# Head B's key blocks paired like head A's, and one block-diagonal product for both last blocks of a row tile

## The chip, the core and the metric

The kernel runs on one core of a Trainium2 chip. A core has a matrix engine (TensorE, PE in the profile; PEld is its loading of weights), a vector engine (VectorE, DVE), a scalar engine (ScalarE, ACT), a general engine (GpSimd, POOL) and a queue engine that only issues DMAs here (SyncE, SP). Each runs its own list of instructions in order, and they wait for each other through semaphores. On-chip memory is SBUF (128 partitions) and PSUM, into which PE writes. The metric is the time of one execution on the device, in microseconds.

## What is computed

Block-causal attention over 8 batches, 8 heads, 576 tokens and 64 channels, then a top-1 mixture of 8 experts. Cut to what matters:

```python
scores = q @ k.T / sqrt(64)                  # per batch and head, 576 x 576
mask   = block_i >= block_j                  # blocks of 64 tokens
attn   = softmax(where(mask, scores, -1e9))
x      = (attn @ v), heads side by side      # 4608 x 512
e      = argmax(x @ w_gate)                  # one expert a token
out    = gate * sigmoid(x @ w_output_gate)[e] * (relu(x @ w1[e]) @ w2[e])
```

The change lies in `attn @ v`. With blocks of 64 tokens, a query block i attends to key blocks 0 to i.

## The kernel before

**Pairs and weaves.** Two heads, A and B, of one batch make a pair; there are 32. The loop at L936 runs one `advance` a pair: it weaves the generators `softmax` of pair p, `flip` of pair p-1 and `values` of pair p-2, one round after another (a `yield` ends a round), and with them what stands in `later`: the loading of q and k for coming units of two pairs (`load_heads`), and a batch's `finish_batch`. This text calls one such pass weave p. PE's order is exactly that of the code. The other engines' lists come from a scheduler that weighs priorities, so an edit in one place can move their rows elsewhere.

**Row tiles.** Queries go in five row tiles: tile 0 holds block 0 (64 rows), tile t holds blocks 2t-1 and 2t (128 rows). `softmax` computes the scores of each tile against its 2t+1 key blocks, takes maxima on DVE (L351, L372, L383), scales them to biases (L327, L385) and writes the exponentials by ACT (L334) into `pt`: 64(2t+1) columns of A, then as many of B. PSUM for scores (`ps_s`) has two buffers.

**Transposes.** `flip` transposes `pt` in squares of 128 columns on PE (L402) and copies them into `pT` by ACT and DVE (L410). The columns fall into pairs of blocks: A's (0,1), (2,3), ..., then one mixed square, A's last block 2t beside B's block 0, then B's pairs (1,2), (3,4), .... So A has a block left at the end, B one at the start.

**Products with v.** `values` has the mixed squares first. v of the two heads comes for them in tiles padded with zeros: `vma` (rows 0 to 63 hold A's blocks 0, 2, 4, 6, 8, the others are zero) and `vmb` (rows 64 to 127 hold B's block 0). L417 and L418 are tile 0's, L421 is one product of 512 columns for B, L423 four of 128 for A. Then the pairs: `va` and `vb`, four products each, over 512, 384, 256 and 128 columns (L430, L434). A's results go to partitions 0 to 63, B's to 64 to 127; each product uses half of the array's columns, and an A and a B product run side by side. All sums gather in `ps_a`, which has one buffer; L441 copies it out, L419 the first tile's.

**Loads.** `load_v` issues four DMAs a pair on SP's queue, in runs of 256 bytes: va and vb (128 KB each), vma (80 KB), vmb (16 KB). The same queue carries q and k (`nat`, L91), their transposes by DMA (L102), the swapped copy of the keys (`sw`, L107 and L108), which the scores need, and the stores of x (L463). Between load and transpose, q and k are split into two f16 halves by DVE (L96) and POOL (L97).

**The batch's end.** `finish_batch` scales rows, routes tokens and ends in five indirect DMAs issued by POOL (L561, the scatters), ahead of the next splits in POOL's list.

Of the kernel before, what the change touches and what calls it, by code (L numbers as in the profile page):

```python
# [10 lines left out]
F32 = mybir.dt.float32  # L11
I32 = mybir.dt.int32
U32 = mybir.dt.uint32
AF = mybir.ActivationFunctionType
# [6 lines left out]
P = 128  # L21
# [5 lines left out]
def block_attention_top1_moe(  # L27
# [11 lines left out]
    nc = tc.nc  # L39
# [3 lines left out]
    NP = H // 2  # L43
# [155 lines left out]
    with tc.high_priority(offset=3000):  # L199
# [11 lines left out]
        vmb = [const.tile([P, D], F32, name=f"vmb{i}") for i in range(3)]  # L211
        vma = [const.tile([P, NT, D], F32, name=f"vma{i}") for i in range(3)]
        for i in range(3):
            nc.gpsimd.memset(vmb[i][0:64], 0.0)
            nc.gpsimd.memset(vma[i][64:128], 0.0)
# [82 lines left out]
    def load_v(b, hp):  # L298
        hA = 2 * hp
        par = (b * NP + hp) % 3  # L300
        va = sb.tile([P, 4, D], F32, name="va", bufs=3)
        vb = sb.tile([P, 4, D], F32, name="vb", bufs=3)
        nc.sync.dma_start(va, v[b, hA, 0:512].rearrange("(j p) d -> p j d", p=P))
        nc.sync.dma_start(vb, v[b, hA + 1, 64:576].rearrange("(j p) d -> p j d", p=P))
        nc.sync.dma_start(vma[par][0:64], v[b, hA].rearrange("(n p) d -> p n d", p=64)[:, 0:9:2, :])
        nc.sync.dma_start(vmb[par][64:128], v[b, hA + 1, 0:64])
        return va, vb, vma[par], vmb[par]

    def softmax(b, hp, stacks, h0, sums, probs):
# [19 lines left out]
        def exps(t, pieces):  # L329
            r, n = ROWS[t], NK[t]  # L330
            if t not in probs:
                probs[t] = sb.tile([P, 2 * n], F32, name=f"pt{t}")
            for ab, ap in pieces:
                last_exp[0] = nc.scalar.activation(  # L334
                    probs[t][0:r, ab * n:(ab + 1) * n], ap, AF.Exp,
                    bias=nbs[0:r, t, ab:ab + 1], scale=SCALE,
                    accum_out=sums[0:r, t, hA + ab:hA + ab + 1],
                )
# [52 lines left out]
    def flip(probs, pT):  # L391
# [4 lines left out]
        for g0 in range(0, len(slots), 4):  # L396
            grp = slots[g0:g0 + 4]
            ps = ps_t.tile([P, 512], F32, name="ps_t").rearrange("p (a n) -> p a n", n=P)
            for i, (t, r) in enumerate(grp):
                rows = ROWS[t]  # L400
                col = t if r == 0 else ((r - 1) // 2 if r % 2 else t + r // 2)
                nc.tensor.transpose(  # L402
                    ps[:, i, 0:rows], probs[t][0:rows, P * col:P * col + P], ident[0:rows, 0:rows]
                )
# [9 lines left out]
    def values(hp, pT, va, vb, vma, vmb, xT):  # L414

        pm = ps_t.tile([P, 512], F32, name="ps_t")
        nc.tensor.matmul(pm[0:64, 0:64], vma[:, 0, :], pT[:, 0, 0:64], start=True, stop=True)  # L417
        nc.tensor.matmul(pm[64:128, 0:64], vmb, pT[:, 0, 0:64], start=True, stop=True)  # L418
        nc.any.tensor_copy(xT[:, hp, 0:64], pm[:, 0:64])  # L419
        pa = ps_a.tile([P, 512], F32, name="ps_a")  # L420
        nc.tensor.matmul(pa[64:128, :], vmb, pT[:, 0, 64:576], start=True, stop=False)  # L421
        for t in range(1, NT):
            nc.tensor.matmul(  # L423
                pa[0:64, P * (t - 1):P * t], vma[:, t, :], pT[:, 0, Q0[t]:Q0[t] + P],
                start=(t == 1), stop=False,
            )
        yield
        yield
        for j in range(4):
            nc.tensor.matmul(  # L430
                pa[0:64, P * j:512], va[:, j, :], pT[:, 1 + 2 * j, 64 + P * j:576],
                start=False, stop=(j == 3),
            )
            nc.tensor.matmul(  # L434
                pa[64:128, P * j:512], vb[:, j, :], pT[:, 2 + 2 * j, 64 + P * j:576],
                start=False, stop=(j == 3),
            )
            if j % 2:
                yield
                yield  # L440
# [657 lines left out]
```

## Time and profile before

| | us |
|---|---|
| median of 3 runs (835.05 to 836.78) | 835.87 |
| the profiled execution | 833.94 |
| its span, first to last instruction | 831.9 |
| PE busy | 777.9 |
| VectorE busy | 547.4 |
| ScalarE busy | 517.4 |
| GpSimd busy | 261.1 |

```profile
## 2 busy tenths in 40 slices
PE   5599999999999999889996999999999999999995
...
DMA  8999889799999899983158499685789968822611
```

The slices are 20.8 us each: the first twenty are attention, the rest the experts. Each digit is the busy share in tenths. Rows of a time line give the start from the beginning of the span, the duration, engine, line, operation, output<-inputs, and in brackets how long the engine had been idle before and what ended that. Group rows give a count, the sum and the mean in ns. A window row gives its bounds, its length, the busy time and instructions of PE, PEld, DVE, ACT and POOL, PE's granted clock, the DMA share and GB/s.

### The profile page before, as it was taken

What the parts mean: (1) busy time and instruction counts of PE and PEld (TensorE: products, weight loads), DVE (VectorE), ACT (ScalarE), POOL (GpSimd) and SP (SyncE); (2) the same over time, 40 slices, a digit from 0 to 9 for tenths busy, and PEclk for the clock granted to TensorE, in tenths of its full rate; (3) what the DMA queues carried; (4) which work ended last, traced back from release to release, by engine and by line L of the source; (5) the groups of instructions that cost most, each with busy time, mean ns of one, the idle gap of its engine ahead of it and who ended that gap; (6) DMA issues with size and microseconds to landing.
All of it is one profiled execution on the core that took longest, in us unless ns stands there. A gap on an engine that the chain in (4) does not pass through costs nothing. (4 is left out here: it accounts for less than half of the span.)

```text
span 831.9 us, 17237 instructions
## 1 busy us (share of the span) xinstructions
PE 777.9 (94%) x6214; PEld 523.5 (63%) x6238; DVE 547.4 (66%) x1188; ACT 517.4 (62%) x1210; POOL 261.1 (31%) x233
## 2 busy tenths in 40 slices
PE   5599999999999999889996999999999999999995
PEld 3366666666676666555673766676656666776652
DVE  6467777878687777758561766786567656786540
ACT  4478786877778777666312855775555555775530
POOL 4322142424232243473236462223123222300001
PEclk9699999999999999999999999999999999999998
DMA  8999889799999899983158499685789968822611
GB/s 156 199 179 171 185 153 194 153 188 191 183 201 175 181 184 200 183 268 107 33 165 208 119 316 303 209 236 114 235 268 290 292 182 210 234 48 57 220 40 41
DMA packets 267053, 151.21 MB, mean 182 GB/s; under 512 B 235600, under 2 KB 235664, under 8 KB 266960
## 3 DMA queue, kind: packets, MB, share of 16 engines
q1 hardware_dynamic: 258688, 130.74, 68.6%
q0 software_dynamic: 8272, 19.29, 7.8%
q8 instruction: 51, 0.84, 0.4%
q14 instruction: 42, 0.34, 0.2%
HBM read 124.33 MB, written 19.73 MB: 173 GB/s over the span
## 5 line engine op out<-in xcount | busy, mean ns | idle before, releaser
L873 PEld LDWEIGHTS <-w1b 128*128 128x128 f16 (+1 forms) x2112 | 184.0, 98 | 26.5 <-issue 3.2
L873 PE MATMUL ps_s<-xt,w1b 128*128 128x256 f16 (+3 forms) x1824 | 182.1, 261 | 0.5 <-DVE w1b L763 0.4
L334 ACT ACTIVATE pt<-ps_s,nbs 128x448 f32<-128x448 f32 (+1 forms) x314 | 163.8, 531 | 23.9 <-DVE nbs L327 10.0
L900 PE MATMUL ps_t<-w2b,hh 128*128 128x512 f16 (+1 forms) x584 | 175.8, 379 | 2.3 <-ACT hh L881 2.3
L763 DVE TENSOR_TENSOR w2b<-w2f,w2b 128x1024 bf16<-128x1024 f32 x76 | 88.0, 1221 | 114.2 <-ACT w2b L762 114.2
L410 ACT COPY pT<-ps_t 128x512 f32<-128x512 f32 (+3 forms) x221 | 97.8, 463 | 74.1 <-PE ps_t L402 73.1
L402 PE MATMUL ps_t<-ident,pt 128*128 128x128 f32 (+1 forms) x800 | 133.0, 287 | 2.5 <-DVE xn L459 2.4
L900 PE MATMUL ps_t<-w2b,hl 128*128 128x512 f16 x304 | 115.2, 379 | 1.7 <-DVE hl L882 0.6
L97 POOL TENSOR_TENSOR sp<-nat,sp 128x1152 f16<-128x1152 f32 x30 | 71.2, 2375 | 145.1 <-DVE sp L96 111.2
L903 ACT ACTIVATE ys<-ps_t,ids 128x512 f32<-128x512 f32 x38 | 26.0, 688 | 137.7 <-PE ps_t L900 91.5
L319 PE MATMUL ps_s<-tr,tr 128*128 128x448 f16 (+1 forms) x378 | 99.6, 286 | 6.4 <-ACT pt L334 6.0
L900 PEld LDWEIGHTS <-hh 128*128 128x128 f16 x608 | 59.2, 98 | 69.2 <-ACT hh L881 2.8
L904 POOL DMA_INDIRECT out_dram<-ys,ids x38 | 43.4, 1143 | 185.2 <-ACT ys L903 134.5
L320 PE MATMUL ps_s<-sw,tr 128*128 128x448 f16 (+1 forms) x378 | 92.2, 286 | 9.4 <-DMA sw<-tr 9.4
L402 PEld LDWEIGHTS ps_t<-ident,pt 128*128 128x128 f32 (+1 forms) x800 | 87.8, 143 | 18.4 <-issue 5.5
L763 DVE TENSOR_TENSOR w1b<-w1f,w1b 128x1024 bf16<-128x1024 f32 x76 | 88.0, 1221 | 0.2 <-ACT w1b L762 0.2
L434 PE MATMUL ps_a<-pT,vb 128*64 128x512 f32 (+3 forms) x256 | 83.5, 450 | 0.0
L430 PE MATMUL ps_a<-pT,va 128*64 128x512 f32 (+3 forms) x256 | 83.5, 450 | 0.0
L372 DVE TENSOR_REDUCE nmx<-ps_s 128x2 f32<-128x896 f32 (+1 forms) x63 | 60.2, 956 | 32.7 <-PE ps_s L322 32.5
L762 ACT CAST w1b<-w1f 128x1024 f16<-128x1024 f32 x76 | 74.0, 1044 | 0.3 <-DMA w1f<-in_moe_w_dram 0.2
L762 ACT CAST w2b<-w2f 128x1024 f16<-128x1024 f32 x76 | 73.6, 1042 | 0.0
L736 POOL DMA_INDIRECT xg<-x_d,ids x38 | 55.3, 1455 | 53.5 <-DMA ids<-tab_d 20.6
(196 smaller groups left out, 1122.0 us busy)
## 6 DMA issues: line engine op xcount, KB each, us to landing
w1f<-in_moe_w_dram SPq DMA_DIRECT2D x76, 512.0 KB
w2f<-in_moe_w_dram SPq DMA_DIRECT2D x76, 512.0 KB
nat<-in_k_dram SPq DMA_DIRECT2D x15, 576.0 KB
nat<-in_q_dram SPq DMA_DIRECT2D x15, 576.0 KB
sw<-tr SPq DMA_DIRECT2D x30, 288.0 KB
x_d<-xn SPq DMA_DIRECT2D x32, 256.0 KB
va<-in_v_dram SPq DMA_DIRECT2D x32, 128.0 KB
vb<-in_v_dram SPq DMA_DIRECT2D x32, 128.0 KB
```

What stands on the lines that cost most here:

```text
L97: last_lo[0] = lo.tensor_tensor(sp[:, :, 1, :], self.nats[i], sp[:, :, 0, :], ALU.subtract)
L319: nc.tensor.matmul(ps_ap, qq, k1[ab][:, c0:c1], start=True, stop=False)
L320: nc.tensor.matmul(ps_ap, qq, k2[ab][:, c0:c1], start=False, stop=last)
L334: last_exp[0] = nc.scalar.activation(probs[t][0:r, ab * n:(ab + 1) * n], ap, AF.Exp, bias=nbs[0:r, t, ab:ab + 1], scale=SCALE, accum_out=s ...
L402: nc.tensor.transpose(ps[:, i, 0:rows], probs[t][0:rows, P * col:P * col + P], ident[0:rows, 0:rows])
L410: copies[next(nth)](pT[:, r:r + m, Q0[t]:Q0[t] + rows], ps[:, i:i + m, 0:rows])
L430: nc.tensor.matmul(pa[0:64, P * j:512], va[:, j, :], pT[:, 1 + 2 * j, 64 + P * j:576], start=False, stop=(j == 3),)
L434: nc.tensor.matmul(pa[64:128, P * j:512], vb[:, j, :], pT[:, 2 + 2 * j, 64 + P * j:576], start=False, stop=(j == 3),)
L762: nc.scalar.copy(hi, src)
L763: eng.tensor_tensor(lo, src, hi, ALU.subtract)
L873: nc.tensor.matmul(ph[:, f4].rearrange("p (h n) -> p h n", n=P), wv[:, cc, f, :], xv[:, cc], start=(k == 0), stop=(k == 3 * KD - 1))
L900: nc.tensor.matmul(py, hv[:, f, h], wv[:, f, :], start=(k == 0), stop=(k == 3 * KF - 1))
```

## The change

B's exponentials are written with their blocks in reverse order, so that B's last block 2t lands beside A's last block 2t in the mixed square, and B's pairs become (2j+1, 2j), the same pairs as A's. `vb` is loaded with its two halves exchanged to match, by two DMAs of 64 KB.

The mixed square of tile t then needs only the rows of query block 2t, 64 columns of `pT` (the other query block of the tile does not see block 2t). It is multiplied with a 128x128 tile `vd`: A's block 2t in its upper left quarter, B's in its lower right, zeros elsewhere. So one product of 64 columns gives both heads at once, in place of L421's 512 columns and L423's four times 128. Of `vd`, blocks 0, 2, 4 and 6 are copied on chip from `va` and `vb` by POOL, two copies a pair; block 8 comes by two DMAs of 16 KB. `vd` has two tiles, where `vma` and `vmb` had three. A pair has five DMAs for v, 288 KB, where it had four, 352 KB.

In `values` the pairs now come first (j = 0, then 1 to 3 together), and the products with `vd` last, each with its copy out of PSUM right behind.

```diff
@@ -208,11 +208,11 @@
         mneg = const.tile([P, 64], BF16, name="mneg")
         nc.vector.memset(mneg, 0.0)
         nc.vector.memset(mneg[0:1], -1e30)
-        vmb = [const.tile([P, D], F32, name=f"vmb{i}") for i in range(3)]
-        vma = [const.tile([P, NT, D], F32, name=f"vma{i}") for i in range(3)]
-        for i in range(3):
-            nc.gpsimd.memset(vmb[i][0:64], 0.0)
-            nc.gpsimd.memset(vma[i][64:128], 0.0)
+        vd = [const.tile([P, NT, P], F32, name=f"vd{i}") for i in range(2)]
+        for i in range(2):
+            nc.gpsimd.memset(vd[i][0:64, :, 64:128], 0.0)
+            nc.gpsimd.memset(vd[i][64:128, :, 0:64], 0.0)
         ones16 = const.tile([P, P], F16, name="ones16")
@@ -297,14 +297,26 @@
     def load_v(b, hp):
         hA = 2 * hp
-        par = (b * NP + hp) % 3
         va = sb.tile([P, 4, D], F32, name="va", bufs=3)
         vb = sb.tile([P, 4, D], F32, name="vb", bufs=3)
+        vA, vB = (v[b, hA + x].rearrange("(n p) d -> p n d", p=64) for x in range(2))
         nc.sync.dma_start(va, v[b, hA, 0:512].rearrange("(j p) d -> p j d", p=P))
-        nc.sync.dma_start(vb, v[b, hA + 1, 64:576].rearrange("(j p) d -> p j d", p=P))
-        nc.sync.dma_start(vma[par][0:64], v[b, hA].rearrange("(n p) d -> p n d", p=64)[:, 0:9:2, :])
-        nc.sync.dma_start(vmb[par][64:128], v[b, hA + 1, 0:64])
-        return va, vb, vma[par], vmb[par]
+        for x in range(2):
+            nc.sync.dma_start(vb[64 - 64 * x:128 - 64 * x], vB[:, x:8:2, :])
+        diag = vd[(b * NP + hp) % 2]
+        nc.sync.dma_start(diag[0:64, 4, 0:64], vA[:, 8, :])
+        nc.sync.dma_start(diag[64:128, 4, 64:128], vB[:, 8, :])
+        def copies():
+            for i in range(3):
+                yield
+            nc.gpsimd.tensor_copy(diag[0:64, 0:4, 0:64], va[0:64])
+            yield
+            nc.gpsimd.tensor_copy(diag[64:128, 0:4, 64:128], vb[64:128])
+        later.append(copies())
+        return va, vb, diag
     def softmax(b, hp, stacks, h0, sums, probs):
@@ -331,8 +343,13 @@
             if t not in probs:
                 probs[t] = sb.tile([P, 2 * n], F32, name=f"pt{t}")
             for ab, ap in pieces:
+                to = probs[t][0:r, ab * n:(ab + 1) * n]
+                if ab:
+                    to = to.rearrange("p (i c) -> p i c", c=64)[:, ::-1, :]
+                    ap = ap.rearrange("p (i c) -> p i c", c=64)
                 last_exp[0] = nc.scalar.activation(
-                    probs[t][0:r, ab * n:(ab + 1) * n], ap, AF.Exp,
+                    to, ap, AF.Exp,
                     bias=nbs[0:r, t, ab:ab + 1], scale=SCALE,
                     accum_out=sums[0:r, t, hA + ab:hA + ab + 1],
                 )
@@ -398,10 +415,10 @@
             ps = ps_t.tile([P, 512], F32, name="ps_t").rearrange("p (a n) -> p a n", n=P)
             for i, (t, r) in enumerate(grp):
                 rows = ROWS[t]
-                col = t if r == 0 else ((r - 1) // 2 if r % 2 else t + r // 2)
-                nc.tensor.transpose(
-                    ps[:, i, 0:rows], probs[t][0:rows, P * col:P * col + P], ident[0:rows, 0:rows]
-                )
+                j = (r - 1) // 2
+                col = P * t if r == 0 else (P * j if r % 2 else P * (2 * t - j))
+                nc.tensor.transpose(ps[:, i, 0:rows], probs[t][0:rows, col:col + P], ident[0:rows, 0:rows])
             i = 0
             while i < len(grp):
                 t, r = grp[i]
@@ -411,33 +428,26 @@
                 i += m
             yield
-    def values(hp, pT, va, vb, vma, vmb, xT):
+    def values(hp, pT, va, vb, diag, xT):
+        pa = ps_a.tile([P, 512], F32, name="ps_a")
+        for j in range(4):
+            for a in range(2):
+                nc.tensor.matmul(
+                    pa[64 * a:64 * a + 64, P * j:512], (va, vb)[a][:, j, :], pT[:, 1 + 2 * j + a, 64 + P * j:576],
+                    start=(j == 0), stop=False,
+                )
+            if j in (0, 3):
+                yield
+                yield
         pm = ps_t.tile([P, 512], F32, name="ps_t")
-        nc.tensor.matmul(pm[0:64, 0:64], vma[:, 0, :], pT[:, 0, 0:64], start=True, stop=True)
-        nc.tensor.matmul(pm[64:128, 0:64], vmb, pT[:, 0, 0:64], start=True, stop=True)
-        nc.any.tensor_copy(xT[:, hp, 0:64], pm[:, 0:64])
-        pa = ps_a.tile([P, 512], F32, name="ps_a")
-        nc.tensor.matmul(pa[64:128, :], vmb, pT[:, 0, 64:576], start=True, stop=False)
+        nc.tensor.matmul(pm[:, 0:64], diag[:, 0, :], pT[:, 0, 0:64], start=True, stop=True)
         for t in range(1, NT):
             nc.tensor.matmul(
-                pa[0:64, P * (t - 1):P * t], vma[:, t, :], pT[:, 0, Q0[t]:Q0[t] + P],
-                start=(t == 1), stop=False,
+                pa[:, P * t - 64:P * t], diag[:, t, :], pT[:, 0, P * t:P * t + 64], start=False, stop=(t == NT - 1),
             )
-        yield
-        yield
-        for j in range(4):
-            nc.tensor.matmul(
-                pa[0:64, P * j:512], va[:, j, :], pT[:, 1 + 2 * j, 64 + P * j:576],
-                start=False, stop=(j == 3),
-            )
-            nc.tensor.matmul(
-                pa[64:128, P * j:512], vb[:, j, :], pT[:, 2 + 2 * j, 64 + P * j:576],
-                start=False, stop=(j == 3),
-            )
-            if j % 2:
-                yield
-                yield
+        nc.any.tensor_copy(xT[:, hp, 0:64], pm[:, 0:64])
         nc.any.tensor_copy(xT[:, hp, 64:576], pa)
     scatters, tab_reads = [], []
```

PE's list in weave 17, before: behind the first scores (L322 ends them) and the first four transposes stand the products of the mixed square; behind them the next scores.

```order
L322 MATMUL ps_s<-mneg,mrow 128x64
L402 MATMUL ps_t<-ident,pt_2919 128x64
L402 MATMUL ps_t<-ident,pt_2916 128x128 x3
L417 MATMUL ps_t<-pT,vma_99 64x64
L418 MATMUL ps_t<-pT,vmb_96 64x64
L421 MATMUL ps_a<-pT,vmb_96 64x512
L423 MATMUL ps_a<-pT,vma_99 64x128 x4
L319 LDWEIGHTS tr_2546
```

After, at the end of the same weave's fifth round (L334 is the mask's product, L421 now the transposes):

```order
L334 LDWEIGHTS mrow
L334 MATMUL ps_s<-mneg,mrow 128x64
L421 MATMUL ps_t<-ident,pt_3001 128x128 x4
L445 MATMUL ps_t<-pT,vd_97 128x64
L447 MATMUL ps_a<-pT,vd_97 128x64 x4
L421 MATMUL ps_t<-ident,pt_3001 128x128 x5
```

The place of L417 to L423 is taken by the two 512-column products of va and vb; the mixed squares stand four rounds later, in five products that fill all 128 output partitions.

DVE's list where weave 15 ends and weave 16 begins, before (L351 is the first maximum of weave 16; the copy of `ps_a`, L441, is on ACT here, in weave 15):

```order
L383 TENSOR_REDUCE nmx<-ps_s 128x1
L459 TENSOR_TENSOR xn<-ps_t,rec 128x512
L385 TENSOR_SCALAR nbs<-nmx 128x1
L541 SCALAR_TENSOR_TENSOR sl<-er,rank 128x5
L556 SCALAR_TENSOR_TENSOR zs<-zs,se 128x5
L543 TENSOR_SCALAR sli<-sl 128x5
L557 RECIPROCAL idg<-zs 128x5
L410 COPY pT<-ps_t 128x128
L351 TENSOR_REDUCE nmx<-ps_s 128x2
```

After, at the same place (L368 is that maximum, L339 its biases, L451 the copy of `ps_a`):

```order
L400 TENSOR_REDUCE nmx<-ps_s 128x1
L469 TENSOR_TENSOR xn<-ps_t,rec 128x512
L402 TENSOR_SCALAR nbs<-nmx 128x1
L553 TENSOR_SCALAR sli<-sl 128x5
L368 TENSOR_REDUCE nmx<-ps_s 128x2
L368 TENSOR_REDUCE nmx<-ps_s 64x2
L339 TENSOR_SCALAR nbs<-nmx 128x1 x2
L339 TENSOR_SCALAR nbs<-nmx 64x1 x2
L451 COPY xT<-ps_a 128x512
L427 COPY pT<-ps_t 128x128
```

The copy of weave 15's sums now stands behind the maxima and biases of weave 16. The same holds at weaves 12, 20, 24 and 28; in nearly all others DVE has it ahead of them, with the first tile's copy (L450) one row before the last bias.

POOL's list around the scatters of weave 16, before:

```order
L481 MEMSET lh 64x128
L552 TENSOR_TENSOR z<-L,oh 128x40
L561 DMA tab_d<-idg,sli 37120x2 x5
L942 MEMSET sums 128x8
L97 TENSOR_TENSOR sp<-nat,sp 128x18x64 x4
```

After (L571 are the scatters, L314 and L316 the copies of pair 14):

```order
L491 MEMSET lh 64x128
L562 TENSOR_TENSOR z<-L,oh 128x40
L314 COPY vd_96<-va 64x4x64
L571 DMA tab_d<-idg,sli 37120x2 x5
L316 COPY vd_96<-vb 64x4x64
L952 MEMSET sums 128x8
L97 TENSOR_TENSOR sp<-nat,sp 128x18x64 x2
```

One copy stands ahead of the scatters, one between them and the splits of the next unit.

## The prediction

> **What bounds the kernel now.** I read the busy times by stage first, then the time line of TensorE (PE) in one weave, then the waits. A weave p is one pass of the attention loop: softmax of head pair p, transposes of pair p-1, products with v of pair p-2; there are 32 pairs.
>
> ```profile
> core 0: us, PE busy (x) PEld busy (x) DVE busy (x) ACT busy (x) POOL busy (x), PEclk, DMA share, GB/s
> 0.00:42.00 42.00, 21.42 (x143) 14.49 (x145) 23.36 (x66) 18.30 (x55) 18.01 (x35) 0.82 0.96 178
> 42.00:320.00 278.00, 273.04 (x2381) 180.53 (x2379) 208.98 (x635) 214.70 (x716) 85.45 (x67) 1.00 0.95 181
> 320.00:410.00 90.00, 80.46 (x660) 52.30 (x653) 60.26 (x187) 57.19 (x168) 41.28 (x32) 0.94 0.69 160
> 410.00:832.00 422.00, 403.00 (x3043) 276.17 (x3065) 254.81 (x300) 227.25 (x274) 116.35 (x100) 0.99 0.65 188
> ```
>
> From 42 to 320 us PE is busy 273.04 of 278.00 us: time taken off PE there is time off the end, as long as nothing else is late. VectorE (DVE) and ScalarE (ACT) have a quarter of that stretch free, but the DMA share is 0.95, so the loads are the second candidate. From 320 to 410 us PE idles 9.5 us. The last 422 us are experts work, which the change does not touch and which starts when attention hands over, so I let it shift as a block.
>
> **What goes and what comes on PE.** All products with v in weaves 16 and 17, by the time line of PE (start, duration):
>
> ```profile
> 209.94 0.27 PE L417 MATMUL ps_t<-pT,vma 128*64 128x64 f32 x1
> ...
> 211.08 0.31 PE L319 MATMUL ps_s<-tr,tr 128*128 128x320 f16 x1
> ...
> 212.98 0.63 PE L402 MATMUL ps_t<-ident,pt 128*128 128x128 f32 x4
> 213.54 0.64 PE L430 MATMUL ps_a<-pT,va 128*64 128x512 f32 x1
> ...
> 215.20 0.39 PE L319 MATMUL ps_s<-tr,tr 128*128 128x512 f16 x1
> ...
> 217.28 0.43 PE L430 MATMUL ps_a<-pT,va 128*64 128x256 f32 x1
> ...
> 218.08 0.77 PE L402 MATMUL ps_t<-ident,pt 128*128 128x128 f32 x5
> ```
>
> Ends overlap, so I count from start to start. The group with the last blocks (L417 to L423) takes 209.94 to 211.08 = 1.14 us. The group j = 0, 1 takes 215.20 - 213.54 = 1.66 us for two passes of 512 + 384 columns (the A and B halves run side by side), the group j = 2, 3 takes 0.80 us for two of 256 + 128. The difference, 0.86 us for 1024 columns, is 0.84 ns a column; what is left, 0.80 - 768 x 0.00084 = 0.155 us, is paid once by each group that uses half of the array's columns. There is also an entry: four transposes last 0.63 us from 212.98 with the last one 0.27 long, so that one starts at 213.34 and the group 0.20 later, where transposes follow each other at (0.63 - 0.27) / 3 = 0.12. That is 0.08 more a group.
>
> After, va and vb have the same columns in two groups instead of three, so the old group goes whole: 1.14 + 0.08 = 1.22 us. In its place stand five products of 64 columns with 128x128 weights, two passes each: ten passes. The streaming is 64 x 0.84 = 0.054 us a pass. The weights load beside it:
>
> ```profile
> 211.66 0.14 PEld L402 LDWEIGHTS ps_t<-ident,pt 128*128 128x128 f32 x1
> ```
> ```profile
> 211.66 0.20 PEld L402 LDWEIGHTS ps_t<-ident,pt 128*128 128x128 f32 x2
> ```
>
> Two such loads end 0.06 us apart, so the port takes one every 0.06 us. No row has f32 passes of 64 columns with 128-column weights one after another. Low end: 0.054 (stream alone); high end: 0.12, the spacing of the 128-column transposes, if load and stream do not overlap. I take 0.058, since at 128 columns the load is wholly covered (0.12 is near the stream's 0.108): ten passes are 0.58 us. **Gain on PE: 1.22 - 0.58 = 0.64 us a pair, 20.5 us for 32.**
>
> The Trainium skill speaks against this: "TensorE: Matmul & The Clock Gate", LDWEIGHTS (loading the stationary operand), gives the load as columns over 1.2 in ns, an estimate of 107 ns for 128 columns, and its section The mechanism lets a load overlap a running product only in another row group. By that page a pass is at least 0.107 us, the gain 0.15 us a pair at most, and with the charges below the time 836.4 or later; the two rows above, 0.06 apart, do not bear out the first rule, and no row tests the second at 64 columns. It is the third rival's case.
>
> **What the new order costs.** `values` now starts with va and vb into ps_a, and ps_a has one buffer. In four weaves that count (12, 16, 20, 24; 28 comes ahead of a wait that I price below) DVE has the copy of ps_a behind the reduces and biases of the next softmax. The same work in weave 17:
>
> ```profile
> 208.67 0.19 PE L319 MATMUL ps_s<-tr,tr 128*128 128x64 f16 x1
> 208.69 0.19 PE L320 MATMUL ps_s<-sw,tr 128*128 128x64 f16 x1
> ```
> ```profile
> 208.21 0.69 DVE L441 COPY xT<-ps_a 128x512 f32<-128x512 f32 x1 [0.36 <-PE ps_a L434]
> 208.87 0.29 DVE L410 COPY pT<-ps_t 128x128 f32<-128x128 f32 x1
> 209.37 0.74 DVE L351 TENSOR_REDUCE nmx<-ps_s 128x2 f32<-128x384 f32 x2 [0.21 <-PE ps_s L322]
> 210.04 0.31 DVE L327 TENSOR_SCALAR nbs<-nmx 128x1 f32<-128x1 f32 x4
> ```
>
> The biases end 210.35 - 208.67 = 1.68 us into the weave; with 0.69 for the copy ps_a is free at 2.37. PE wants it where the old group started, 209.94 - 208.67 = 1.27. The stall is 1.1 us, four times; 0 at the least, 2.1 if one more copy of 0.69 and one of 0.29 come first. I take 1.1, since the order names no such copy. In ordinary weaves the copy ends 0.23 us into the weave; the pm copy now ahead of it (0.29, by the 128-column pT row) makes that 0.5, covered until 1.27. The 0.29 also delays the last bias and its exp; the score buffer that this exp frees is wanted at 211.08, 2.4 us into the next weave.
>
> The exps of head B write the same elements in reversed blocks; no row has that. Below: nothing; above: one more 0.2 us a piece, 0.8 a weave. ACT has 63 us free in 278, so I take nothing on the path.
>
> **Copies on GpSimd (POOL).** 64 copies of 64x256. Bounds:
>
> ```profile
> 191.60 0.26 POOL L552 TENSOR_TENSOR z<-L,oh 128x40 f32<-128x40 f32 x1 [2.72 <-DVE oh L517]
> ```
> ```profile
> L763 POOL TENSOR_TENSOR w1b<-hh,w1b 128x1024 bf16<-128x1024 f32 x2 | 4.3, 2144 | 0.6 <-ACT w1b L762 0.6
> ```
>
> 0.26 is the floor, 2.14 the ceiling; scaled by 256 of 1024 elements it is 0.54, and I take 0.5. POOL has room (85 of 278 busy), but one chain has none:
>
> ```profile
> 198.38 0.94 POOL L561 DMA_INDIRECT tab_d<-idg,sli  x1 [6.53 <-DVE idg L557]
> ...
> 205.50 4.71 POOL L97 TENSOR_TENSOR sp<-nat,sp 128x1152 f16<-128x1152 f32 x2
> ```
> ```profile
> 207.91 5.59 SPq L102 DMA_TRANSPOSE tr<-sp  x2
> ...
> 214.19 0.58 SPq L108 DMA_DIRECT2D sw<-tr  x1
> ```
> ```profile
> 219.62 0.20 PE L320 MATMUL ps_s<-sw,tr 128*128 128x64 f16 x1 [0.74 <-DMA sw<-tr]
> ```
> ```profile
> PE ps_s L320 <- DMA sw<-tr: 0.7, 1, 0.7
> ```
>
> At the start of weave 16 the scatters begin (198.38), then the two splits, transposes and swap for the unit that weave 18 needs: 21.24 us, and PE waits 0.74 for it. PE's two weaves shrink by 2 x 0.64 - 1.1 = 0.2, and one copy now stands between scatters and splits: 0.5. That is 0.7 us more wait at weave 18. The last row, from the waits of 40 to 400 us, says that this is the only such wait; weaves 14, 22 and 26 have the same chain, so I charge 0 there, with 0.7 each as the upper bound.
>
> **The late loads.** In weave 29:
>
> ```profile
> 357.47 0.30 PE L417 MATMUL ps_t<-pT,vma 128*64 128x64 f32 x2 [4.28 <-DMA vma<-in_v_dram]
> ```
> ```profile
> 342.50 4.74 SPq L102 DMA_TRANSPOSE tr<-sp  x1
> ...
> 351.52 0.67 SPq L305 DMA_DIRECT2D vma<-in_v_dram  x1
> 352.23 0.62 SPq L306 DMA_DIRECT2D vmb<-in_v_dram  x1
> ```
>
> PE waits here for loads of pair 27, whose queue (SyncE) goes back through transposes, splits and loads to the scatters of weave 24. This point moves by what those scatters gain: 22 pairs x 0.64 = 14.1, less 3 x 1.1 (weaves 12, 16, 20), less 0.7, less 0.5 for the copy in this chain: 9.6. A fifth DMA a pair adds 0.62 us (vmb's row) on that queue for pairs 24 to 26, 1.9; 64 KB less a pair at 181 GB/s gives back 0.36 each, 1.1. I charge 0.8 and get 8.8. What pairs 22 to 26 gain is lost in this wait. Behind it, pairs 27 to 31 keep 5 x 0.64 = 3.2. **Sum: 12.0 us.** The profiled execution took 833.94 (span 831.9), 1.93 below the median of the runs, 835.87; forecast 821.9 for it and **823.9** for the median.
>
> **The rivals.**
> Everything lands: the stalls on ps_a and the loads shift with PE, because their sources are PE's own results; 20.5 us, 815.4. Against it: the 4.28 us wait, and ps_a's place on DVE. Chance 0.12.
>
> The loads set the pace: the DMA share of 0.95 and PE's wait of 0.74 say that they stand just behind PE. Then the point in weave 29 hardly moves, and only pairs 27 to 31 pay (3.2) plus what 64 KB less a pair frees: between 0 and a third of 28 x 0.36. Gain 3 to 7, 829 to 833. Against it: splits and scatters follow DVE, which follows PE. Chance 0.2.
>
> Slower: the weights do not load beside 64-column passes. A pass is then 0.12, the gain a pair 1.22 - 1.20 = 0.02, 0.5 for the 27 pairs that count, and of the charges 3.3 + 0.5 + 0.8 = 4.6 stay: 4.1 slower, 840.0. It decides at 4.6 / 27 = 0.17 a pair, a pass of 0.105. Against it: the 64-column f16 scores, with a load each, start 0.02 apart (208.67, 208.69), shorter than any load shown. Chance 0.08.
>
> **How the numbers follow.** Forecast 0.6 (its own range 819 to 828, by the bounds of stall, copy and pass); the rest as above. The range must hold 8 in 10: with most of the second rival, and short of the first and third, 816 to 832. About 0.2% (1.7 us) is what a measurement can tell from no change. Faster by more: 0.58 + 0.12 + 0.18 = 0.88; within: 0.02 + 0.02 + 0.01 = 0.05; slower: 0.07.
>
> **What would show it.** The five products with vd should start 0.055 to 0.06 us apart per pass; at 0.1 the third rival holds. ps_a's first product should wait some 1.1 us for DVE in weaves 12, 16, 20 and 24 and nowhere else. The swap wait at weave 18 should be 1.4, and weave 29 should still wait for va or vb, longer than 4.28. No wait for vd itself: its copies end behind the scatters, about 8 us into the weave, and PE comes there at 8.5 or later. A wait for vd in each fourth weave, or POOL copies above 1.5 us, would prove me wrong, and so would a time line in which SyncE never waits for POOL.

## The result, and the profile after

The changed kernel is slower: 880.61 us (median of 4 runs, 879.88 to 882.0) against 836.26 (4 runs, 835.05 to 836.78), a ratio of 1.053, 95% interval 1.0511 to 1.0547. The forecast was 823.9, so it failed in sign. The profiled execution has a span of 880.4 us.

The windows of the changed kernel, in the columns of before, with the bound behind attention at 460 in place of 410:

```profile
42.00:320.00 278.00, 252.70 (x2023) 169.62 (x2022) 189.87 (x593) 185.00 (x615) 90.18 (x103) 0.96 0.81 153
320.00:460.00 140.00, 119.32 (x921) 81.23 (x921) 84.64 (x259) 83.29 (x253) 60.98 (x60) 0.93 0.73 146
460.00:880.00 420.00, 399.42 (x3011) 271.82 (x3033) 252.04 (x295) 226.70 (x272) 117.12 (x100) 0.99 0.64 188
```

The experts' part is about as long as it was (420 and 422 us by these windows; from its first product, L873 and now L883, to the end 365.8 and now 366.9); the loss lies in attention. PE now idles 25 of the 278 us where it idled 5, and its granted clock is 0.96 where it was 1.00. The waits of PE from 40 to 470 us (total, times, longest) name two new ones:

```profile
PE ps_t L445 <- POOL vd L316: 26.1, 6, 5.8
PE ps_s L332 <- DMA sw<-tr: 12.4, 6, 9.2
PE ps_t L534 <- ACT pT L427: 3.7, 5, 1.0
```

Of the sw waits, 9.2 us are one wait at the start, which the kernel before has too (8.7, up to 39.6 us, just ahead of this window). The waits for vd are the change's own: one of 5.0 to 5.8 us in each of weaves 12, 16, 20 and 24, and two late ones of 2.0 and 3.0 in weaves 28 and 29. The five weaves 12, 16, 20, 24 and 28 together took 51.5 us before and take 94.9 now, so 43.4 of the 48.5 us between the two spans lie there. One batch in both kernels, before and after (weaves 16 to 19):

```profile
198.07:245.13 47.06, 45.25 (x398) 29.91 (x396) 34.85 (x110) 36.06 (x119) 16.07 (x13) 1.00 0.94 179
```
```profile
208.54:264.35 55.81, 48.20 (x381) 32.44 (x379) 36.29 (x114) 34.31 (x113) 18.11 (x20) 0.94 0.81 150
```

The batch has grown by 8.75 us: PE's idle time went from 1.81 to 7.61, and PE is busy 2.95 us longer with 17 instructions fewer. GpSimd's time line shows why it waits:

```profile
209.75 0.39 POOL L314 COPY vd<-va 64x256 f32<-64x256 f32 x1 [6.42 <-DMA va<-in_v_dram]
210.44 0.95 POOL L571 DMA_INDIRECT tab_d<-idg,sli  x1 [0.30 <-DVE nmx L368]
...
215.55 0.97 POOL L571 DMA_INDIRECT tab_d<-idg,sli  x1 [0.30 <-issue]
224.19 0.40 POOL L316 COPY vd<-vb 64x256 f32<-64x256 f32 x1 [7.67 <-DMA tab_d<-idg,sli]
224.65 0.10 POOL L952 MEMSET sums<- 128x8 f32 x1
224.84 2.36 POOL L97 TENSOR_TENSOR sp<-nat,sp 128x1152 f16<-128x1152 f32 x1
```

Read the brackets. The upper left copy (L314) stands ahead of the scatters and waits for va to land. The lower right copy (L316) stands behind them, and is held until the five scatters have landed, 7.67 us after the last was issued. The splits of q and k stand behind that. The list of the built program says the same: each first copy into partitions 64 to 127 behind a batch's scatters waits for their five semaphores (DMASW), a copy into partitions 0 to 63 never does, not even where it stands behind them. So the wait was written into the program when it was built. Why it is put there for one half only, no run here shows.

```
L571 DMA tab_d<-idg,sli 37120x2 x4
L316 COPY vd_96<-vb 64x4x64 [waits DMASW3_49,DMASW2_49,DMASW7_49,DMASW1_49,DMAHW3_49,DMASW0_49,Pool_49]
```

PE's time line and windows at the same place:

```profile
209.47 0.41 PE L445 MATMUL ps_t<-pT,vd 128*128 128x64 f32 x2 [0.26 <-ACT pT L427]
209.71 1.06 PE L447 MATMUL ps_a<-pT,vd 128*128 128x64 f32 x8
210.60 0.72 PE L421 MATMUL ps_t<-ident,pt 128*128 128x128 f32 x5
...
224.65 0.69 PE L445 MATMUL ps_t<-pT,vd 128*128 128x64 f32 x2 [5.00 <-POOL vd L316]
225.12 1.91 PE L447 MATMUL ps_a<-pT,vd 128*128 128x64 f32 x8
```
```profile
224.60:227.90 3.30, 3.25 (x16) 3.19 (x16) 0.98 (x3) 0.83 (x2) 2.46 (x2) 0.50 0.00 0
227.90:232.00 4.10, 4.10 (x30) 2.58 (x29) 2.90 (x10) 2.19 (x10) 2.76 (x3) 0.83 0.77 144
```

Two things are to be seen. At full clock the ten passes with vd take 210.60 - 209.47 = 1.13 us, not 0.58. And behind the 5.00 us wait the clock is 0.50 for 3.3 us: the same ten passes take 2.18 (224.65 to 226.83, where the next transposes start). A window from 222.50 to 229.20 has a clock of 0.50 throughout; 4.55 us of it are PE's work, and half of those, 2.3 us, are most of the 2.95 us of longer busy time.

### The profile page after: what moved, and what is told of

It reads as the page before. It is cut to its first block, busy times and chain, and to the rows that moved or that the text cites. A ratio compares the mean times of both kernels' runs of the same rounds, so it can differ in the third digit from the quotient of the medians.

```text
span 880.4 us, 17188 instructions
## 1 busy us (share of the span) xinstructions
PE 791.2 (90%) x6086; PEld 536.0 (61%) x6110; DVE 548.9 (62%) x1206; ACT 513.1 (58%) x1192; POOL 285.5 (32%) x295
## 5 line engine op out<-in xcount | busy, mean ns | idle before, releaser
L883 PEld LDWEIGHTS <-w1b 128*128 128x128 f16 (+1 forms) x2112 | 182.6, 98 | 25.8 <-DVE w1b L773 2.3
L351 ACT ACTIVATE pt<-ps_s,nbs 128x448 f32<-128x448 f32 (+1 forms) x314 | 163.9, 530 | 45.6 <-DVE nbs L402 25.3
L883 PE MATMUL ps_s<-xt,w1b 128*128 128x256 f16 (+3 forms) x1824 | 182.3, 261 | 1.1 <-DVE w1b L773 1.1
L427 ACT COPY pT<-ps_t 128x512 f32<-128x512 f32 (+3 forms) x221 | 99.8, 469 | 103.0 <-PE ps_t L421 98.4
L421 PE MATMUL ps_t<-ident,pt 128*128 128x128 f32 (+1 forms) x800 | 136.0, 292 | 6.4 <-DVE xn L469 3.3
L331 PE MATMUL ps_s<-tr,tr 128*128 128x448 f16 (+1 forms) x378 | 101.8, 291 | 7.7 <-ACT pt L351 6.9
L332 PE MATMUL ps_s<-sw,tr 128*128 128x448 f16 (+1 forms) x378 | 94.0, 290 | 12.4 <-DMA sw<-tr 12.4
L914 POOL DMA_INDIRECT out_dram<-ys,ids x38 | 46.7, 1230 | 178.7 <-ACT ys L913 116.4
L421 PEld LDWEIGHTS ps_t<-ident,pt 128*128 128x128 f32 (+1 forms) x800 | 92.2, 149 | 20.3 <-ACT pT L427 6.1
L746 POOL DMA_INDIRECT xg<-x_d,ids x38 | 52.8, 1389 | 53.6 <-DMA ids<-tab_d 23.5
```

Source lines behind the costliest of these rows:

```text
L331: nc.tensor.matmul(ps_ap, qq, k1[ab][:, c0:c1], start=True, stop=False)
L332: nc.tensor.matmul(ps_ap, qq, k2[ab][:, c0:c1], start=False, stop=last)
L351: last_exp[0] = nc.scalar.activation(to, ap, AF.Exp, bias=nbs[0:r, t, ab:ab + 1], scale=SCALE, accum_out=sums[0:r, t, hA + ab:hA + ab + 1],)
L421: nc.tensor.transpose(ps[:, i, 0:rows], probs[t][0:rows, col:col + P], ident[0:rows, 0:rows])
L427: copies[next(nth)](pT[:, r:r + m, Q0[t]:Q0[t] + rows], ps[:, i:i + m, 0:rows])
L883: nc.tensor.matmul(ph[:, f4].rearrange("p (h n) -> p h n", n=P), wv[:, cc, f, :], xv[:, cc], start=(k == 0), stop=(k == 3 * KD - 1))
```

## The experiments

Each kernel was timed against the kernel before on the same chip. Chips differ: before took 860 to 861 us where e1 to e8 and e18 ran, 835 to 837 where e9 to e17 did; ratios are quoted, and only those of one kind of chip are set against each other.

### Where the copies stand

e1 moves both copies to ACT; e2 moves the one from vb alone, e3 the one from va alone; e4 drops them and loads the whole diagonal.

```diff
 e1
-            nc.gpsimd.tensor_copy(diag[0:64, 0:4, 0:64], va[0:64])
+            nc.scalar.copy(diag[0:64, 0:4, 0:64], va[0:64])
-            nc.gpsimd.tensor_copy(diag[64:128, 0:4, 64:128], vb[64:128])
+            nc.scalar.copy(diag[64:128, 0:4, 64:128], vb[64:128])
 e4, with no copies
-        nc.sync.dma_start(diag[0:64, 4, 0:64], vA[:, 8, :])
-        nc.sync.dma_start(diag[64:128, 4, 64:128], vB[:, 8, :])
+        nc.sync.dma_start(diag[0:64, :, 0:64], vA[:, 0:9:2, :])
+        nc.sync.dma_start(diag[64:128, :, 64:128], vB[:, 0:9:2, :])
```

> Both copies into vd run on ACT in place of GpSimd. Theory (GpSimd's queue): of the 44 us that the change costs, the vd waits of weaves 12, 16, 20, 24 and what follows from them (late splits and loads, the low clock behind each stall) make about 4 x 9.6 us and another 6 in weaves 28 and 29; without copies on GpSimd they go, the steady gain of 0.2 us a weave (weave 5: 10.02 before, 9.80 after) stays: 836 - 32 x 0.2 = 829.5 us, 825 to 835; PE waits for vd under 2 us in all. Rival 1 (the new order of the products, with va and vb first into the one ps_a, or the fifth load a pair, is what costs): 865 to 881. Rival 2 (ACT is as bad a place, since its queue holds the exps behind a copy that waits for va to land): 840 to 860, with ACT waiting for the va and vb loads by tens of us.

> Only the copy from vb into vd's lower right quarter moves to ACT; the one from va stays on GpSimd, ahead of the scatters as before. Theory A (the lower right copy, which stands behind a batch's five scatters and waits until they have landed, is the main cause): under 840 us, GpSimd still waits for va ahead of the scatters. Theory B (the copy from va, which holds the scatters and the splits behind them until va lands, 6.4 us at 209.75, is the main cause): over 860 us, with the sw waits grown to several us each fourth weave.

> The other way round: the copy from va on ACT, the one from vb into the lower right quarter on GpSimd, behind the scatters. Theory A: 860 to 880 us, since its wait for the scatters to land stays (7.7 us at 224.19); the scatters themselves begin 1.6 us earlier at the most (they wait for DVE next), so PE's waits for vd go from 5 to some 3.5 us a batch. Theory B: under 840 us.

> No copies at all: the two small loads of block 8 into vd become loads of all five diagonal blocks from DRAM, 128 KB more a pair. Theory (GpSimd's queue): the vd waits of each batch go, as with the copies on ACT. By bytes the loads take 128 KB / 181 GB/s = 0.7 us more a pair on the 16 DMA engines: 829 us if hidden, up to 829 + 32 x 0.7 = 852 if the loads set the pace. Rival 1 (order of the products): 865 us or more.

Measured: e1 1.011 (1.0079 to 1.0141), e2 1.0125 (1.0071 to 1.0179, two runs), e3 1.0385 (1.0352 to 1.0418, two runs), e4 1.0279 (1.0253 to 1.0306). From the waits of PE in e2, then e3, and of ACT in e1:

```profile
PE ps_t L445 <- POOL vd L314: 0.3, 1, 0.3
```
```profile
PE ps_t L445 <- POOL vd L316: 7.7, 5, 3.3
```
```profile
ACT vd L314 <- DMA va<-in_v_dram: 13.0, 5, 7.6
```

The upper left copy on GpSimd costs nothing that shows (e2 against e1); the lower right one costs 2.7% (e3 against e1). That is theory A's order and not theory B's. The figures that both gave were for a chip on which before takes 836 us. As ratios to that, e3 lies in A's range, while e2 misses both ranges: A had it under 1.005, B over 1.029, with sw waits that grew, and they did not (12.2 us in e2, 11.4 in e1).

All of them stay slower than before. e1, forecast at 829.5 us or 0.99, lies by its ratio in the range of its rival 2, the copies on ACT in front of the exps; e9 and e11 below speak against that one. e4, with no copy at all but 128 KB more a pair, is slower than e1: the expectation of 852 us at the most was too low in ratio as well. PE waited 24.3 us for sw there (six waits, 7.9 of it at the start). So there is a second cause; that it sits with the loads is shown further down, by e14.

### Both kernels on the slower chip

e5 is the kernel before, e6 the changed one, word for word.

> The kernel before, for its trace beside those of this call: a chip can differ from another in its speed (the kernel before took 836 us on one and 861 us on another). If the chip is as the first, 836 us and waits for vma of 4.3 us in weave 29; if it is as the second, 861 us, and the trace shows where 25 us more lie.

> The changed kernel, for its trace beside the one of before on the same chip. Theory (GpSimd's queue) and every rival: 1.053 times before if a chip's speed scales both; where the chip has late loads of its own, less, since a wait for vd then stands beside another wait.

e5 took 860.96 us, e6 884.88: 1.028 (1.0205 to 1.0364, two runs of e6). The first wait of PE in e5:

```profile
PE ps_s L319 <- ACT pt L334: 18.2, 11, 3.8
```

On this chip the kernel before has a stall of its own, for ACT's exps, in weaves 8, 12, 16, 20 and 24: weave 16 takes 16.23 us where it took 10.59. The change's waits fall into the same weaves, and its waits for vd come to 12.3 us in e6, where they were 26.1: part of them seems to be hidden behind the stall. Why that chip has the stall is open, and so is why e3 came out above e6, which has one copy more on GpSimd.

### The pass of the products with vd

e7 is e1 with four groups of products added behind those with vd, whose results nobody reads.

```diff
+        for n in (64, 128):
+            for i in range(4):
+                nc.tensor.matmul(pm[:, 128:128 + n], diag[:, i, :], pT[:, 0, 0:n], start=True, stop=True)
+        for i in range(4):
+            for a in range(2):
+                nc.tensor.matmul(
+                    pm[64 * a:64 * a + 64, 256:320], diag[:, i, 64 * a:64 * a + 64], pT[:, 0, 0:64], start=True, stop=True
+                )
+        for i in range(4):
+            nc.tensor.matmul(pm[0:64, 320:384], diag[:, i, 0:64], pT[:, 0, 0:64], start=True, stop=True)
```

> The copies on ACT, as in e1, and behind the five products with vd four groups of products that nobody reads, into unused columns of the same bank: four of 64 columns with the 128-column weights of vd, four of 128 columns with the same weights, four pairs of 64 columns with 64-column weights side by side in the two halves of the array, four of 64 columns with 64-column weights in one half. In the trace of after a pass of 64 columns takes 0.107 to 0.113 us. If loading 128 columns of weights sets that pace and hides nothing behind a shorter stream, the four 64-column products take 8 x 0.107 = 0.86 us, the 128-column ones 8 x 0.108 to 0.12 = 0.86 to 0.96, and the single halves with half the weights 8 x 0.054 to 0.06 = 0.43 to 0.48. If a pass is load and stream one after the other, with 0.054 each, the 128-column ones take 8 x 0.16 = 1.3. If it is a fixed cost of any pass, all forms take the same 0.86.

e7's time line of PE:

```profile
198.56 1.06 PE L447 MATMUL ps_a<-pT,vd 128*128 128x64 f32 x8
199.45 2.00 PE L452 MATMUL ps_t<-pT,vd 128*128 128x64 f32 x16
201.38 0.69 PE L455 MATMUL ps_t<-pT,vd 128*64 128x64 f32 x16
201.90 0.63 PE L459 MATMUL ps_t<-pT,vd 128*64 128x64 f32 x8
202.46 0.33 PE L421 MATMUL ps_t<-ident,pt 128*128 128x128 f32 x1
```

The eight passes of L447 take 0.89 us, 0.111 each. L452 is eight passes of 64 columns and eight of 128 (the time line joins them): 1.93 us for 16, and single starts lie 0.112 apart in both halves. The eight double passes of L455, with half the weights in each half of the array, take 0.52; inside the group they start 0.058 apart. This is the first of the three cases that were expected. The 128 columns of weights set the pace, with 64 streamed columns as with 128; with 64 columns of weights it is half, and two halves go side by side for the price of one. Load and stream do overlap, for the passes of 128 streamed columns take no longer; but where the stream is shorter, the load is the floor.

By the Trainium skill, "TensorE: Matmul & The Clock Gate", section LDWEIGHTS (loading the stationary operand), 128 columns take an estimate of 107 ns and K rows do not matter; the f32 passes here agree (0.112 and, with 64 columns, 0.058; 0.058 as well with the 64 rows of e9 below).

### The order, and the form of the products

e8 is the kernel before with va and vb first and the last blocks last. e9 needs no vd: A's last blocks already lie in rows 0 to 63 of va, B's in rows 64 to 127 of vb, so each tile gets two products of 64 rows and 64 columns in opposite corners of the array. e10 has them right behind j = 0. e11 is e1 with vd's halves side by side.

```diff
 e9
+        ve = sb.tile([P, D], F32, name="ve", bufs=3)
+        nc.sync.dma_start(ve[0:64], vA[:, 8, :])
+        nc.sync.dma_start(ve[64:128], vB[:, 8, :])
...
+                h = slice(64 * a, 64 * a + 64)
+                nc.tensor.matmul(
+                    pa[h, P * t - 64:P * t] if t else pm[h, 0:64], ve[h] if t == 4 else (va, vb)[a][h, t, :],
+                    pT[h, 0, P * t:P * t + 64], start=(t == 0), stop=(t in (0, 4)),
+                )
```

> The kernel before with one part of the change alone: the products with va and vb first and the last blocks at the end of the weave, with the old products, loads and buffers. Theory (GpSimd's queue): within 1% of before. Rival 1 (the late place of the last products, which frees va, vb and the accumulators later and puts the copies of xT behind the next softmax): 1.01 or more of before, with PE waiting for ACT's exps and for sw as in e1.

> No vd at all: A's last blocks stand in rows 0 to 63 of va and B's in rows 64 to 127 of vb, so each row tile's last blocks are two products of 64 rows and 64 columns, straight from va and vb (block 8 from one small tile with three buffers), side by side in two corners of the array. No copies, no zeros, no wait for vd; four loads of v a pair but for one more small one. If the pass of 64-column weights side by side is 0.058 us as in e7 (201.55 to 201.84: 0.29 for five), the group takes 10 x 0.058 + 0.2 to begin = 0.8 against 1.22 of before: 0.4 a weave, 13 us in all if nothing else is late. Theory (GpSimd's queue and the 0.112 pass make the loss): faster than before by 4 to 13 us, 0.985 to 0.995. Rival (the late loads and the exps set the pace whatever PE does): 0.995 to 1.005.

> As e9, with the last blocks' products right behind the first products with va and vb instead of at the end of the weave: one group of half-array products less (0.2 us a weave), and the accumulators and the copies of xT come free about as early as before the change. If late frees cost something, 3 to 8 us faster than e9; if not, the 0.2 us a weave alone, up to 6.

> e1 (the copies into vd on ACT) with each 128-column product split into its two 64-column halves, side by side, on the same vd: only the form of the last blocks' products differs from e1. By e7 a weave's ten passes go from 1.12 to 0.58 us plus 0.2 to begin: 0.3 a weave, up to 10 us less than e1 (1.011 of before), so 1.000 to 1.006 of before where PE sets the pace; 1.011 again if it doesn't.

Measured: e8 1.0024 (1.0002 to 1.0046), e9 1.0163 (1.0127 to 1.02), e10 1.0166 (1.0108 to 1.0224), e11 1.0157 (1.0123 to 1.019). On e8's chip the order costs next to nothing. That chip has the stall of the section before, which may hide a part; on the faster kind e9 and e10, with the last blocks late and early, have the same ratio, but the order was not tried alone there. The corner products do what they should: weave 5, where nothing waits, takes 10.02 us before, 9.81 in the changed kernel and 9.61 in e9:

```profile
71.93:81.95 10.02, 10.02 (x89) 6.66 (x87) 6.79 (x20) 8.21 (x28) 1.05 (x1) 1.00 1.04 196
```
```profile
72.92:82.73 9.81, 9.81 (x86) 6.79 (x83) 6.64 (x21) 8.08 (x27) 0.79 (x2) 1.00 0.99 194
```
```profile
73.90:83.51 9.61, 9.61 (x95) 6.36 (x93) 6.76 (x21) 7.97 (x28) 0.00 (x0) 1.00 0.96 191
```

Yet e9 to e11 lose 1.6%, with no copy on GpSimd left; e9 and e11 miss both of the ranges expected for each, and what e10 gains on e9 is not clear of the spread of its runs (844.41 to 853.84). e9 has no copies at all and e11 both on ACT, and they are equal: copies on ACT cost nothing that shows. e11 also gives the price of those on GpSimd: its weaves 12, 16, 20, 24 and 28 take 63.4 us together, where the changed kernel's take 94.9. e9's waits name the loads (of the first line, 8.9 us are the wait at the start, which before has too):

```profile
PE ps_s L316 <- DMA sw<-tr: 13.8, 4, 8.9
PE ps_a L420 <- DMA va<-in_v_dram: 6.9, 3, 2.8
```

### The loads of v

e12 is e10 with block 8 of both heads in one load, so four a pair; e13 issues that load on ACT's queue. e14 is the kernel before with its load of vb cut in two, and nothing else. e15 is e10 with three loads. e16 is the kernel before, its pairs and order kept, with one load of v a pair.

```diff
 e14
-        nc.sync.dma_start(vb, v[b, hA + 1, 64:576].rearrange("(j p) d -> p j d", p=P))
+        for x in range(2):
+            nc.sync.dma_start(
+                vb[64 * x:64 * x + 64], v[b, hA + 1, 64:576].rearrange("(j x p) d -> x p j d", x=2, p=64)[x]
+            )
 e16
-        nc.sync.dma_start(va, v[b, hA, 0:512].rearrange("(j p) d -> p j d", p=P))
-        nc.sync.dma_start(vb, v[b, hA + 1, 64:576].rearrange("(j p) d -> p j d", p=P))
-        nc.sync.dma_start(vma[par][0:64], v[b, hA].rearrange("(n p) d -> p n d", p=64)[:, 0:9:2, :])
-        nc.sync.dma_start(vmb[par][64:128], v[b, hA + 1, 0:64])
+        vv = sb.tile([P, 9, D], F32, name="vv", bufs=3)
+        nc.sync.dma_start(vv, v[b, hA:hA + 2].rearrange("h s d -> (h s) d").rearrange("(n p) d -> p n d", p=P))
...
-                pa[0:64, P * (t - 1):P * t], vma[:, t, :], pT[:, 0, Q0[t]:Q0[t] + P],
+                pa[0:64, P * (t - 1):P * t], vv[0:64, t, :], pT[0:64, 0, Q0[t]:Q0[t] + P],
```

> e10 with block 8 of both heads in one load, so four loads of v a pair, as many as before the change. Theory (the fifth load): SyncE's queue is at work 42.8 of 47.1 us in the batch from 198.07 of before, so a load more (0.6 to 0.8 us a pair, 2.5 to 3 a batch of four weaves) makes the loads late, and PE waits for va (6.0 us in e10) and loses its clock. With four loads the waits for va and vb go (under 2 us), and the shorter products show: 0.99 of before, 0.985 to 1.0. Rival (the loads are late for another reason, such as the two halves of vb on half the partitions, or the new place of the products): 1.01 to 1.017, as e10.

> e12 with this one small load issued on ACT's queue, so SyncE issues three loads a pair. Theory (the fifth load): as e12 or a little faster, 0.98 to 0.995, if ACT has room for 32 issues. Rival: the same as e12 within 0.3%, since three or four no longer matter.

> The kernel before with one part of the change alone: the load of vb cut into two loads of 64 partitions each, the same bytes; so five loads a pair. Theory (the fifth load): 1.005 to 1.02 of before, with new waits of PE for vma, va or sw. Rival: within 0.3% of before.

> e10 with three loads of v a pair on SyncE's queue and none elsewhere: A's 640 rows (its block 8 in the upper half of the fifth place) in one, B's five even blocks and its four odd ones in one each. Theory (the number of loads on SyncE's queue is the second cause): no waits of PE for va or vb, 0.99 to 1.003 of before (e12 with four loads 1.007, e10 with five 1.017); what is left over is PE's wait for ACT's exps, 14.6 us in e12. Rival (loads of 64 partitions are slow in themselves): 1.007 or more.

> The kernel before with its pairs, its order and its exps, but v of both heads in one load a pair (1152 rows as nine times 128, 288 KB instead of four loads with 352 KB): block 8 of A and block 0 of B share the fifth place, so the last blocks' products read 64 rows of it, in opposite corners of the array, and the zero-padded tiles go. Theory (the number of loads on SyncE's queue): the waits of before for vma (4.8 us), sw at weave 18 and vmb go, SyncE's queue has 2 us a pair more room: 0.985 to 0.997 of before, faster than every other kernel here. Rival (PE alone sets the pace, 45.25 of 47.06 us busy): within 0.3% of before.

Measured: e12 1.0068 (1.0036 to 1.0101), e13 1.0099 (1.0059 to 1.0139), e14 1.017 (1.013 to 1.0211), e15 1.004 (1.0019 to 1.0061), e16 1.0121 (1.0084 to 1.0158). e14 shows the second cause: a fifth load of v, the same bytes, costs the kernel before some 14 us (1.7%; 11 to 18 by the interval). Its first wait of PE, now in weaves 13, 21, 25 and 29, was 4.8 us before:

```profile
PE ps_t L420 <- DMA vma<-in_v_dram: 12.6, 4, 4.4
```

Four loads in place of five give most of it back (e10 1.017, e12 1.007: the same bytes and the same halves of vb), so the number counts. Between four and three nothing is told, for the intervals of e12 and e15 overlap; and that loads on 64 partitions are slow in themselves is not excluded for the rest. e12, e13, e15 and e16 all miss their expectation, though (e15 by 0.001), and mostly by a wait that moved on. In e13, with the small load on ACT's queue, PE waits 25.0 us for ACT's exps. In e16 no wait for a load is left and SyncE's queue has room. PE's first wait, what DVE's split (L96) waits for, and SyncE's first wait:

```profile
PE ps_s L307 <- ACT pt L322: 18.6, 14, 4.1
```
```profile
  DMA tr<-sp: 23.4, 12
```
```profile
SPq L102 <- PE ps_s L310: 61.9, 11, 11.4
```

The split now comes before the transposes of the unit ahead have freed its buffer, and stands in DVE's list ahead of the biases.

### A third buffer for the split halves

e17 is e16, e18 is e15, each with `bufs=3` on the tile `sp`.

> e16 with a third buffer for the split halves of q and k (sp). In e16 no wait for a load of v is left, but DVE's split, which is in DVE's queue ahead of the next biases, waits for the transposes of the unit before to free its buffer (23.4 us in 12 waits, none before the change), and PE waits 18.6 us for ACT's exps behind it. Theory (that wait gave back what the loads gained): PE's waits for the exps fall under 5 us, 0.985 to 0.997 of before. Rival (the exps are late for another reason, such as GpSimd's scatters or splits beside DVE): 1.005 or more.

> e15 (re-paired, last blocks in opposite corners, three loads a pair) with e17's third buffer for the split halves. Theory (what is left over in e15 is the chain of loads and splits): 0.988 to 0.997 of before, at or under e17's 0.994, since its weaves are 0.4 us shorter where nothing waits. Rival (DVE does not wait for that buffer in e15, its trace shows none, so the third buffer brings nothing there): 1.002 to 1.006, as e15.

Measured: e17 0.9943 (0.9917 to 0.9968), 832.49 us; e18 0.9935 (0.9908 to 0.9962) on the slower kind of chip, 853.51 us against 859.71. Both are a little faster than the kernel before, each in the range expected, and so faster than the changed one; between them nothing is told, since they ran on different chips. The mechanism is shown only in part. In e17's profile, taken of the slowest of its twelve runs (837.9 us), DVE still waits 16.6 us for that buffer and PE 13.3 for the exps, more than the 5 expected. In e18 it is not shown at all: DVE does not wait for that buffer in e15, which has two, and PE waits 21.2 us for the exps in e18. The third buffer alone in the kernel before, with its four loads, was not run; in its trace, too, DVE has no such wait.

## Why the prediction was wrong, step by step

**PE as the bound, loads second.** Right as a reading of before, but the second bound was far closer than it was priced. e14 adds one load and loses 14 us.

**Ten passes of 0.058 us.** This is the first step that failed. A pass takes 0.112, the stalled clock aside. The row that was read as a port's pace, two weight loads 0.06 apart, was no measure of it, and the argument against the third rival took f16 scores, which start 0.02 apart with a load each, for f32 products. The gain was 0.2 us a weave (weave 5: 10.02 to 9.81), not 0.64: 14 of the 20.5 us were never there. The third rival named this mechanism, with a chance of 0.08, but it priced the gain that is left at 0.02 a pair, not 0.2. With 0.2 the prediction's own sum (27 pairs at 0.2, less charges of 5.3) would have come out at no change. So this step took away the gain; it does not make the loss.

**The stall on ps_a, 1.1 us in each of four weaves.** It did not come. In weave 16 the order was as described, and DVE ended the copy at 211.49, but PE reached ps_a only at 212.57, because the vd products of the pair before and nine transposes stand ahead. e8, on the other kind of chip, agrees (1.002).

**The copies on GpSimd at 0.5 us.** The duration was nearly right, 0.39. What failed is the sentence "No wait for vd itself: its copies end behind the scatters, about 8 us into the weave". The prediction asked how long a copy takes and what stands behind it, and not what the copy itself waits for: va's landing for the upper left one, the scatters' landing for the lower right one. The latter ended at 224.59, 16 us into weave 16; PE waited 5.00 us, then ran at half clock. This was named as what would prove the forecast wrong ("A wait for vd in each fourth weave"), but had no price among the rivals. On the faster chip, the changed kernel is at 1.053 and e11, with the copies on ACT, at 1.016. That is 31 us, and the five weaves behind the scatters alone differ by 31.5: some 30 us hang on this step. e11's faster products could save up to 6 us in all (weave 9: 9.61 in place of 9.80), about 1 of them in those five weaves. That it is the lower right copy alone was shown on the slower kind of chip (e2 and e3).

**The fifth load at 0.8 us.** Mis-sized. It was charged for three pairs ahead of one wait, as 0.62 each; alone in the kernel before it costs some 14 us (e14). There it is not one wait: weaves 13, 17, 21 and 25 take 13.0 to 15.7 us each, where each took 10.0 to 10.8, so the queue runs late anew in each batch. The swap wait at weave 18, forecast at 1.4, came out at 0.96 (at 239.44).

**Weave 29.** The wait for late loads of pair 27 that was to grow beyond 4.28 became a wait for vd of 2.96 (at 412.26). Here the lower right copy was held not by the scatters but by a late load, 6.05 us up to 411.81: the forecast wait came by another way.

**The reversed exps at nothing.** Right: ACT's 314 exps take 163.9 us in the changed kernel and 163.8 before.

The missing 57 us (880.6 less 823.9) thus fall apart as some 30 for the copies, 14 for the load and 12 for the passes (27 pairs at 0.44), less the 3.3 of the stall and the 2.0 already charged for copies and load: 51. The parts overlap in the same weaves, so the sum is a check of sizes and no more, and the last 6 us have no cause here.

## What to carry to other kernels

A step put into an engine's list is priced by what it waits for, and then by what stands behind it: here two copies of 0.39 us a pair cost some 30 in all, because one of them waited for other work's DMAs in front of PE's next operand. A queue whose users have no slack has no free place for one more small entry, even with fewer bytes; count the entries and see which wait ends last when they move by one. And a duration is only borrowed from a row of the same type and shape.

## What the runs showed of the hardware

- Passes of f32 products (two a product) with weights of 128 columns start 0.112 us apart with 64 or with 128 streamed columns, with 64 columns of weights 0.058, two halves side by side (e7). 64-row corners of the array, fed from different rows and columns, work side by side as well: in e9 the two products of a tile start within 0.01 us of each other, and such pairs 0.058 apart.
- In the wait of 5.00 us, which began at 219.65, PE's granted clock was 1.00 up to 222.40 and 0.50 from 222.50 to 229.20; from 229.40 on it was 1.00 again. The Trainium skill, "TensorE: Matmul & The Clock Gate", section Part 1: The HAM clock gate (the "warmup" mystery), says that half rate follows an idle window of about 3.4 us and lasts until as long a busy one. These rows are near it and not equal to it: half rate began some 2.8 us after PE fell idle and lasted some 4.6 us after it was busy again.
- Five scatters of at most 128 rows had landed 7.67 us after the last was issued (issued until 216.52, the copy that waits for them freed at 224.19).
- The same kernel took 835 us on some chips and 861 on others. In the traces of the two, weaves 8, 12, 16, 20 and 24 take 5.4 to 6.2 us more each.
